# Infini-attention with a gated mix: when the next segment's x is asked for, and a new table by slot

## The chip, the cores and the metric

The kernel runs on one core of one Trainium2 chip. The metric is the time of one execution on the device in microseconds (us), as the median of several runs; the kernel before has 1017.42 us (three runs, 1017.11 to 1020.25).

## The reference

Two branches A and B with weights of their own read the same x (2048 tokens, 640 wide, 32 heads of 20) and are mixed by a gate for each token. Each branch is attention over four segments of 512 tokens, with a memory that is carried from segment to segment:

```python
phi = lambda t: jnp.where(t > 0, t + 1.0, jnp.exp(t))
for s in range(N):                      # N = 4 segments
    qs, ks, vs = q[:, :, s], k[:, :, s], v[:, :, s]
    logits = jnp.einsum("bhqd,bhkd->bhqk", qs, ks) * scale + mask
    a_dot = jnp.einsum("bhqk,bhkd->bhqd", _softmax(logits, axis=-1), vs)
    pq = phi(qs)
    a_mem = einsum(pq, M) / (einsum(pq, z)[..., None] + 1e-6)
    outs.append(g * a_mem + (1.0 - g) * a_dot)
    M = M + jnp.einsum("bhld,bhle->bhde", phi(ks), vs)
    z = z + phi(ks).sum over l
...
g = _sigmoid((x * gate_w).sum(-1, keepdims=True))
return g * a + (1 - g) * b              # a, b: the branches' outs @ wo
```

The causal mask adds -1e9 above the diagonal. q, k and v are x times 640 x 640 weights.

## The kernel before

**Stages.** A stage t = 0 to 7 is one branch of one segment: segment t // 2, branch A for even t and B for odd t. In each stage the products q, k (five blocks of 128 output columns each, m = 0 to 4), v (two halves of 320 columns, called m = 0 and m = 4) and o (five blocks) are to be computed, in three parts each (high by high, low by high, high by low), all at line 769. x and every weight are therefore split into a high and a low part: ACT copies the high part (x at L582, weights at L537, v's weights at L511), and POOL, or VectorE at the start, subtracts for the low one (L586, L539, L514). v's weights come in three pieces through the three tiles `wst`.

**Attention units.** Each stage has eight units of four heads, 64 in all (i). For a unit, q and k rows are loaded into one of four pairs of tiles (`qst`, `kst`, L1163). L1205 are the scores whose row maxima VectorE takes (L1192); VectorE writes the maxima as two parts (`mt`, L1218 and L1219), TensorE transposes them (L1232), ACT copies them (`mr`, L1249), and a DMA puts them below q (L1244). L1297 are the transposed scores with the maxima subtracted, ACT takes Exp (L1289), POOL clears what the mask hides (L1290), and L1317 multiplies by v. L879 reads the memory and L961 updates it; L921 are transposes.

**How TensorE is shared.** A matmul over 64 rows takes one half of the array, and two of them, one on each half, run beside each other. L1317 takes the whole array, with four products beside each other in column groups.

**What sets the order.** Nothing is decided on the chip. A planner in Python keeps a clock with a length for every operation, a queue for each engine (A is ACT, D is VectorE, G is POOL, S is SyncE, which issues all DMAs) and pools of tiles (34 `row` tiles, eight `bank` tiles in PSUM, three `wst` tiles), and writes each engine's instructions down in the order in which they come out; an engine then runs them in that order, and waits where one isn't ready. The attention units come slot by slot: a slot i issues five T steps of unit i (`t_unit`, L1297) and five S steps of unit i + 2 (`s_unit`, L1205). Between them the product jobs fill TensorE, in the order of a list `jobs`. For stages after the first, a window's jobs are k2, v0, q3, k3, q4, k4, v4, and then the next stage's q0, k0, q1, k1, the o products of the stage before, and the next stage's q2.

**The table.** `RULES` has an entry for some slots; a slot without one goes on with the last. An entry holds the order of S and T steps, and seven numbers: `span` (the share of the slot's time in which its steps are laid), `calm` (how much work VectorE may have waiting for lesser units to start), `lag` (how long the second half of a unit waits for its first), `room` (row tiles that must be free for Exp's outputs), `hold`, `wait` and `wait2` (how long other units wait).

**The requests.** `begin` is called as a job starts. It asks for weights four jobs ahead, and at one place for the next segment's x (`want_x`, five transfers from `in_xT`, L592; each needs three free row tiles and leaves two spare). `fill_gen` asks at another place for x by token (`token_gate`, four transfers from `in_x` into `wst` tiles, L635), of which VectorE makes the gates of the segment (L625).

Of the kernel before, what the change touches and what calls it, by code (L numbers as in the profile page):

```python
# [42 lines left out]
def tile_gated_mix_infini_attn(  # L43
# [44 lines left out]


    RULES = {  # L90
# [56 lines left out]
    }  # L147
    rule = {}
    DONE = {"A": 0.27, "D": 0.26, "G": 0.22, "S": 0.0}
# [428 lines left out]
    def want_x(s, k):  # L578

        def got(hi, lo, st):  # L580
            def landed():
                put("A", 0.515, lambda: nc.scalar.copy(hi, r32(st)), low, prio=6)  # L582

            def low():
                e, eng, cost = ("D", nc.vector, 0.66) if s == 0 else ("G", nc.gpsimd, 1.25)
                put(e, cost, lambda: eng.tensor_tensor(out=lo, in0=r32(st), in1=r32(hi), op=ALU.subtract), end, prio=3)  # L586

            def end():
                big.give(st)
                xs[s, k] = (hi, lo)  # L590

            dma(0.87, lambda: nc.sync.dma_start(  # L592
                out=r32(st), in_=xT[P * k:P * (k + 1), L * s:L * (s + 1)]), landed, prio=need[job_index[2 * s, "q", 0]] - 4 * (s > 0), lat=1.2 if s else 1.1)

        big.want((F32R, F32R, F32), got, prio=4, spare=SPARE if s else 0)
# [75 lines left out]
    def ask_gates(*ts):  # L671
        gates_asked.extend(ts)
        for t in list(gates_asked):
            if t // 2 in gates_ready:
                gates_asked.remove(t)
                gq_store.want(1, lambda q, t=t: put("G", 1.3 if t == 7 else 0.7, lambda: gates(t, q), prio=2), prio=t)
# [843 lines left out]
    def begin(i):  # L1520
        t, kind, m = jobs[i]
        for j in range(i, i + AHEAD + 1):
            stage(j)
        if kind == "q" and m == 2 and t > 1:
            ask_gates(t)
        if kind == "v" and m == 4 and t % 2 and t < 7:
            for k in range(KT):
                want_x(t // 2 + 1, k)

    def fill_gen():  # L1530
        for i, (t, kind, m) in enumerate(jobs):
            begin(i)
            if i == 4:
                for n in range(NB):
                    token_gate(n)
            if kind == "v" and m == 0 and t % 2 and t < 7:
                for n in range(NB * (t // 2 + 1), NB * (t // 2 + 2)):
                    token_gate(n)
            if i < len(HEAD0):
                yield from job_head() if i == 0 else ()  # L1540
                continue
            yield from {"q": lambda: job_qk(t, kind, m), "k": lambda: job_qk(t, kind, m),
                        "v": lambda: job_v(t, m // 4), "o": lambda: job_o(t, m),
                        "early": lambda: job_early(t, m), "last": lambda: job_last(t)}[kind]()

    fill = fill_gen()
    filled = [0.0]
    over = [False]
# [241 lines left out]
```

## Time and profile before

| | us |
|---|---|
| median of the runs | 1017.42 |
| the profiled execution's own time | 1018.35 |
| its span in the trace | 1016.6 |
| TensorE busy with matmuls | 1002.2 (99%) |
| TensorE loading weights (beside them) | 855.9 (84%) |
| VectorE busy | 814.0 (80%) |
| ACT busy | 654.1 (64%) |
| POOL busy | 596.3 (59%) |
| bytes moved | 241.99 MB, 238 GB/s in the mean |

"Busy" is the time in which at least one instruction of the engine was under way, so TensorE is also busy where one half of the array idles. The chain of waits goes back from the last instruction to whatever released each one; shares of it say which work set the end. In lists of waits the three numbers are the sum in us, how often, and the longest. In groups of instructions they are the busy time in us and the mean in ns, then the idle time before them.

### The profile page before, as it was taken

What the parts mean: (1) busy time and instruction counts of PE and PEld (TensorE: products, weight loads), DVE (VectorE), ACT (ScalarE), POOL (GpSimd) and SP (SyncE); (2) the same over time, 40 slices, a digit from 0 to 9 for tenths busy, and PEclk for the clock granted to TensorE, in tenths of its full rate; (3) what the DMA queues carried; (4) which work ended last, traced back from release to release, by engine and by line L of the source; (5) the groups of instructions that cost most, each with busy time, mean ns of one, the idle gap of its engine ahead of it and who ended that gap; (6) DMA issues with size and microseconds to landing.
All of it is one profiled execution on the core that took longest, in us unless ns stands there. A gap on an engine that the chain in (4) does not pass through costs nothing.

```text
span 1016.6 us, 30789 instructions
## 1 busy us (share of the span) xinstructions
PE 1002.2 (99%) x11260; PEld 855.9 (84%) x11260; DVE 814.0 (80%) x2732; ACT 654.1 (64%) x1281; POOL 596.3 (59%) x972
## 2 busy tenths in 40 slices
PE   9999999999999999999999999999999999999998
PEld 7988888878898887998889987788887877888875
DVE  5698889887698769886779888689668898779864
ACT  5376676677657567666766566666666556676572
POOL 4455547765466656757555565656664556656471
PEclk9999999999999999999999999999999999999999
DMA  7998989898797788966787588797667978767431
GB/s 255 307 313 261 290 251 317 253 299 258 243 295 230 238 251 257 296 185 198 217 260 241 181 262 245 219 321 252 176 200 205 288 206 264 238 199 246 139 113 53
DMA packets 148887, 241.99 MB, mean 238 GB/s; under 512 B 13216, under 2 KB 46144, under 8 KB 148416
## 3 DMA queue, kind: packets, MB, share of 16 engines
q1 hardware_dynamic: 148736, 240.03, 77.0%
q8 instruction: 89, 1.46, 0.6%
q14 instruction: 62, 0.51, 0.2%
HBM read 150.83 MB, written 94.65 MB: 241 GB/s over the span
## 4 chain that ended last, share of the span: by engine, by line
PE 86%; DVE 7%; DMA 3%; ACT 1%; issue 1%; SPq 0%; POOL 0%; DVEq 0%; ACTq 0%
PE bank L769 51%; PE bank L1317 12%; PE bank L1297 7%; PE bank L1205 7%; PE bank L961 3%; PE bank L879 3%; PE bank L921 2%; DVE bank L1192 2%; DMA row<-rowg 1%; PE bank L1232 1%; DVE mt L1218 1%; DVE mt L1219 1%; DVE row L735 1%; DVE row L1494 1%; ACT p L1289 1%
## 5 line engine op out<-in xcount | busy, mean ns | idle before, releaser
L1192 DVE CUSTOM_DVE_ANT_0 bank<-bank,tri 128x384 f32<-128x384 f32 (+3 forms) x1024 | 474.5, 519 | 125.3 <-PE bank L1205 99.4
L769 PE MATMUL bank<-row,wh 64*128 64x512 f32 x2308 | 517.6, 404 | 1.1 <-DMA qst<-qd 0.8
L1289 ACT ACTIVATE p<-bank 128x512 f32<-128x512 f32 x566 | 311.1, 600 | 127.2 <-PE bank L1297 95.5
L1290 POOL TENSOR_SCALAR_AFFINE_SELECT p<-p 128x128 f32<-128x128 f32 (+1 forms) x566 | 214.0, 386 | 237.7 <-ACT p L1289 225.4
L769 PEld LDWEIGHTS bank<-row,wh 64*128 64x128 f32 x2308 | 324.8, 185 | 12.3 <-DVE mx L1192 1.2
L769 PE MATMUL bank<-row,wl 64*128 64x512 f32 x1154 | 296.7, 399 | 0.0
L539 POOL TENSOR_TENSOR wl<-wst,wh 128x640 fp32r<-128x640 f32 x115 | 179.4, 1565 | 52.7 <-ACT wh L537 51.9
L1297 PE MATMUL bank<-qst,kst 62*128 62x128 f32 (+3 forms) x1024 | 179.7, 318 | 2.7 <-DVE row L1494 0.7
L1205 PE MATMUL bank<-kst,qst 60*128 60x128 f32 (+3 forms) x1024 | 179.0, 317 | 1.7 <-DVE row L719 0.7
L769 PEld LDWEIGHTS bank<-row,wl 64*128 64x128 f32 x1154 | 174.1, 186 | 5.0
L769 PE MATMUL bank<-wvh,row 64*128 64x320 f32 x1280 | 175.4, 312 | 0.0
L769 PEld LDWEIGHTS bank<-wvh,row 64*128 64x128 f32 x1280 | 148.1, 185 | 1.7 <-ACT p L1289 0.3
L1317 PE MATMUL bank<-p,vst 128*32 128x512 f32 (+3 forms) x1888 | 144.7, 424 | 0.0
L1192 DVE DVE_READ_ACCUMULATOR2_ANT mx<- 128x1 f32 x1024 | 144.6, 141 | 0.0
L1297 PEld LDWEIGHTS bank<-qst,kst 62*128 62x128 f32 x1024 | 132.1, 186 | 11.8 <-DVE mx L1192 1.8
L1205 PEld LDWEIGHTS bank<-kst,qst 60*128 60x128 f32 x1024 | 131.2, 186 | 8.2 <-DVE mx L1192 1.8
L1317 PEld LDWEIGHTS bank<-p,vst 128*32 128x32 f32 x1888 | 58.5, 110 | 83.0 <-issue 59.5
L769 PE MATMUL bank<-wvl,row 64*128 64x320 f32 x640 | 103.4, 311 | 0.0
L537 ACT CAST wh<-wst 128x640 fp32r<-128x640 f32 x119 | 86.3, 740 | 23.5 <-PE bank L769 13.1
L1347 ACT COPY row<-bank 128x512 f32<-128x512 f32 x61 | 35.9, 589 | 95.6 <-PE bank L1317 84.5
L769 PEld LDWEIGHTS bank<-wvl,row 64*128 64x128 f32 x640 | 82.9, 185 | 0.1
L514 POOL TENSOR_TENSOR wvl<-wst,wvh 128x640 fp32r<-128x640 f32 (+1 forms) x48 | 64.0, 1337 | 22.6 <-ACT wvh L511 22.5
(117 smaller groups left out, 1255.2 us busy)
## 6 DMA issues: line engine op xcount, KB each, us to landing
qst<-qd SPq DMA_DIRECT2D x128, 240.0 KB
kst<-kd SPq DMA_DIRECT2D x128, 240.0 KB
qd<-row SPq DMA_DIRECT2D x40, 512.0 KB
kd<-row SPq DMA_DIRECT2D x40, 512.0 KB
dots<-row SPq DMA_DIRECT2D x56, 256.0 KB
wst<-wmix SPq DMA_DIRECT2D x35, 320.0 KB
row<-dots SPq DMA_DIRECT2D x42, 256.0 KB
qd<-row SPq DMA_DIRECT2D x40, 256.0 KB
```

Source lines behind the costliest of these rows:

```text
L514: put("G", 0.77 * n, lambda: nc.gpsimd.tensor_tensor(out=wl[:, a:b, :], in0=w3, in1=r32(wh[:, a:b, :]), op=ALU.subtract), end, prio=4)
L537: put("A", 0.625, lambda: nc.scalar.copy(wh, w3), lambda: put(lo_eng, lo_cost, lambda: lo.tensor_tensor(out=wl, in0=w3, in1=r32(wh), op=AL ...
L539: lambda: lo.tensor_tensor(out=wl, in0=w3, in1=r32(wh), op=ALU.subtract), end, prio=3), prio=6)
L769: return nc.tensor.matmul(bank_of, lhsT=w[ROWS[half]], rhs=x_[ROWS[half]], start=start, stop=stop)
L879: return nc.tensor.matmul(pm[:, a - h0:c - h0, :].rearrange("p h e -> p (h e)"), lhsT=r32(pqTs[t, m][ROWS[half], P * n:P * (n + 1)]), rhs= ...
L1192: put("D", w / 960.0 + 0.105, lambda: nc.vector.tensor_tensor_reduce(out=sc[:, off:off + w], in0=sc[:, off:off + w], in1=tri[:, L - w:], s ...
L1205: lane_ops[half].append((mm(w), lambda pair=pair, qb=qb, off=off, w=w, r=r, sc=sc: nc.tensor.matmul(sc[:, off:off + w], lhsT=q[r, pair, P ...
L1289: put("A", 0.483, lambda: nc.scalar.activation(pt, sc, AF.Exp, scale=SCALE), lambda: (bank.give(sc), put("G", 0.15 + 0.105 * len(todo), la ...
L1290: "G", 0.15 + 0.105 * len(todo), lambda: nc.gpsimd.affine_select(out=blocks, in_=blocks, pattern=[[0, len(todo)], [1, P]], base=0, channel ...
L1297: lane_ops[half].append((mm(w), lambda pair=pair, kb=kb, off=off, w=w, r=r, sc=sc: nc.tensor.matmul(sc[:, off:off + w], lhsT=k[r, pair, P ...
L1317: nc.tensor.matmul(po[32 * j:32 * j + 32, P * kb:], lhsT=vst[t % 2][:, kb, h * E1:h * E1 + 32], rhs=pts[i, n, f][0][:, off:off + w], start ...
L1347: either(0.483, lambda: nc.scalar.copy(r32(oT), po), 0.605, lambda: nc.vector.tensor_copy(r32(oT), po), end, 2)
```

## The change

Two conditions and the whole table:

```diff
     RULES = {
-        0: "TSTSTSTSTS 1.033 2.38 0.30 8 0.0 1.6 1.41",
-        1: "TSTSTSTSTS 0.953 3.71 0.30 8 0.0 2.99 0.36",
-        2: "TTSTSTSTSS 1.010 3.52 0.30 4 0.0 2.63 0.25",
...
+        0: "TTSTSTSTSS 1.010 2.38 0.30 8 0.0 1.6 0.71",
+        1: "TSTTSSTSTS 1.010 2.38 0.30 8 0.0 1.6 0.38",
+        3: "TTSTSTSTSS 0.936 2.38 0.30 8 0.0 1.6 1.55",
...
     }
...
-        if kind == "v" and m == 4 and t % 2 and t < 7:
+        if kind == "q" and m == 4 and t % 2 and t < 7:
             for k in range(KT):
                 want_x(t // 2 + 1, k)
...
-            if kind == "v" and m == 0 and t % 2 and t < 7:
+            if kind == "v" and m == 4 and t % 2 == 0 and t < 6:
                 for n in range(NB * (t // 2 + 1), NB * (t // 2 + 2)):
                     token_gate(n)
```

x of the next segment is asked for two jobs earlier (q4 instead of v4 of branch B's stage), and x by token at the second half of v in branch A's stage instead of the first half of v in branch B's. Lines behind the table stand three further down (L592 becomes L595). The number of instructions of each kind is the same on TensorE and SyncE; on the others a few evacuations change their engine. Three places show how the order moves; names carry the number of the tile.

The first is SyncE's queue in stage 5, where x of segment 3 is asked for. Before:

```order
L521 DMA wst0_142<-in_b_wv_dram 128x640
L521 DMA wst2_144<-in_b_wv_dram 128x640
L748 DMA kd5_110<-row25_12547_10686 128x2x512
L748 DMA kd5_110<-row20_12548_10687 128x512
L521 DMA wst0_142<-in_b_wv_dram 128x320
L592 DMA row30_12683_10795<-in_xT_dram 128x512
L592 DMA row31_12689_10799<-in_xT_dram 128x512
L592 DMA row10_12694_10802<-in_xT_dram 128x512
L592 DMA row5_12699_10805<-in_xT_dram 128x512
L1163 DMA qst3_83<-qd5_102 60x2x512 x2
```

After the change:

```order
L524 DMA wst1_143<-in_b_wv_dram 128x640
L524 DMA wst2_144<-in_b_wv_dram 128x640
L595 DMA row27_12554_10711<-in_xT_dram 128x512
L1247 DMA qst0_80<-mr1_162 2x8x128 x2
L595 DMA row5_12560_10715<-in_xT_dram 128x512
L595 DMA row16_12565_10718<-in_xT_dram 128x512
L595 DMA row8_12570_10721<-in_xT_dram 128x512
L1166 DMA qst3_83<-qd5_102 60x2x512 x2
L1166 DMA kst3_87<-kd5_110 60x2x512 x2
L524 DMA wst1_143<-in_b_wv_dram 128x320
```

The third piece of v's weights (128x320) stood ahead of four x transfers; now it stands behind them and behind four loads of q and k rows.

The second is SyncE's queue where x by token for segment 3 is fetched: before, in stage 5, places 497 to 506 of the queue.

```order
L635 DMA wst1_143<-in_x_dram 128x640
L748 DMA qd5_102<-row29_12109_10288 128x2x512
L748 DMA qd5_102<-row5_12110_10289 128x512
L1362 DMA dots4_121<-row19_12189_10350 128x512
L635 DMA wst0_142<-in_x_dram 128x640
L1244 DMA qst3_83<-mr0_161 2x8x128 x2
L635 DMA wst1_143<-in_x_dram 128x640
L635 DMA wst0_142<-in_x_dram 128x640
L1163 DMA qst2_82<-qd5_102 60x2x512 x2
L1163 DMA kst2_86<-kd5_110 60x2x512 x2
```

After the change, in stage 4, places 450 to 458; the fourth of these transfers stands at place 466.

```order
L638 DMA wst0_142<-in_x_dram 128x640
L638 DMA wst2_144<-in_x_dram 128x640
L1166 DMA qst1_81<-qd4_101 60x2x512 x2
L1166 DMA kst1_85<-kd4_109 60x2x512 x2
L638 DMA wst1_143<-in_x_dram 128x640
L551 DMA wst0_142<-wmix1_131 128x5x128
L1247 DMA qst3_83<-mr0_161 2x8x128 x2
L1365 DMA dots4_121<-row11_10929_9279 128x512
L551 DMA wst2_144<-wmix1_131 128x5x128
```

They now take the `wst` tiles ahead of the o products' weights, and not ahead of a q and k load that waits behind them.

The third is ACT's queue at the cast of v's third piece in stage 5. Before:

```order
L511 CAST wvh_153<-wst2_144 128x640
L511 CAST wvh_153<-wst0_142 128x320
L1347 COPY row20_12752_10849<-bank5_139 128x512
L1249 CAST mr1_162<-bank1_135 32x128
L582 CAST row26_12681_10793<-row30_12683_10795 128x512
```

After:

```order
L585 CAST row28_12558_10713<-row5_12560_10715 128x512
L585 CAST row15_12563_10716<-row16_12565_10718 128x512
L585 CAST row12_12568_10719<-row8_12570_10721 128x512
L756 CAST row31_12795_10879<-bank0_134 128x512
L726 ACTIVATE row20_12797_10881<-bank0_134 128x512
L1292 ACTIVATE p4_12817_10894<-bank5_139 128x512
L1292 ACTIVATE p5_12818_10895<-bank3_137 128x512
L514 CAST wvh_153<-wst1_143 128x320
L1252 CAST mr0_161<-bank7_141 32x128
```

The third piece's cast stood ahead of x's casts and now stands behind four of them (the first is five places further up); the copy of the next maxima (`mr`) stands behind it in both.

103 rows, old and new, of the table RULES are left out of this document.

## The prediction

> **What bounds the kernel now.** I read the page first: the engines' busy shares, the rows of slices, and the chain that ended last.
>
> ```profile
> span 1016.6 us, 30789 instructions
> PE 1002.2 (99%) x11260; PEld 855.9 (84%) x11260; DVE 814.0 (80%) x2732; ACT 654.1 (64%) x1281; POOL 596.3 (59%) x972
> PE   9999999999999999999999999999999999999998
> PEclk9999999999999999999999999999999999999999
> DMA packets 148887, 241.99 MB, mean 238 GB/s; under 512 B 13216, under 2 KB 46144, under 8 KB 148416
> PE 86%; DVE 7%; DMA 3%; ACT 1%; issue 1%; SPq 0%; POOL 0%; DVEq 0%; ACTq 0%
> PE bank L769 51%; PE bank L1317 12%; PE bank L1297 7%; PE bank L1205 7%; PE bank L961 3%; PE bank L879 3%; PE bank L921 2%; DVE bank L1192 2%; DMA row<-rowg 1%; PE bank L1232 1%; DVE mt L1218 1%; DVE mt L1219 1%; DVE row L735 1%; DVE row L1494 1%; ACT p L1289 1%
> ```
>
> TensorE works in every slice at the full granted clock, and 86% of the chain is its own work. The change alters no product, so that work stays; only what stands between the products can move. How much is that? The windows at both ends, and TensorE's waits:
>
> ```profile
> 0.00:25.00 25.00, 22.73 (x139) 18.25 (x141) 12.32 (x25) 14.36 (x28) 10.65 (x25) 1.00 0.76 255
> 1000.00:1017.00 17.00, 12.22 (x86) 9.15 (x78) 7.96 (x14) 1.76 (x3) 0.00 (x0) 0.98 0.22 78
> PE bank L1232 <- DVE mt L1219: 1.6, 4, 0.5
> PE bank L769 <- DMA qst<-qd: 0.8, 1, 0.8
> PE bank L1205 <- DVE row L719: 0.7, 1, 0.7
> PE bank L1297 <- DVE row L1494: 0.7, 2, 0.4
> PE bank L1297 <- ACT mr L1249: 0.5, 1, 0.5
> ```
>
> The second number of a window is PE's busy time. Of 1016.6 - 1002.2 = 14.4 us without a product, 25.00 - 22.73 = 2.3 lie before 25 us and 16.6 - 12.22 = 4.4 behind 1000 us, which leaves 7.7 us in the stream, in pieces of at most 0.8 us, mostly behind VectorE. No row names x or its split as what a product waited for. So the asked-for x is no bottleneck that the change could remove; what it can do is to deal the stream's 7.7 us, and the idle halves of the array, anew.
>
> **The change, part by part.** Nothing is added or removed on TensorE, SyncE or the DMA queues: 9732 matmuls and 940 transfers stand in both programs. Three things move.
>
> *1. x of the next segment.* It is asked for at q's fifth product of an odd t instead of at v's second half. The order shows what that makes of SyncE's queue at segments 2 and 3: the x transfers followed all three pieces of v's weights, and now three or four of them stand ahead of the third piece. Was x late before?
>
> ```profile
> L586 POOL TENSOR_TENSOR row<-row,row x5: 1268/1297/1759, 165.5 to 176.3; 128x512 fp32r<-128x512 f32 x5
> L769 PE MATMUL bank<-wvh,row x80: 301/306/412, 159.7 to 176.4; 64*128 64x320 f32 x80
> ```
>
> These are the tile views of the first such place (150 to 185 us; "first and last start"). The last split of x starts at 176.3 and takes 1.3 us, so x is whole at 177.6; the last v product with wvh starts at 176.4, and products with wvl follow it, of which half as many are in the program. So x was just in time even here, and TensorE has attention units to run meanwhile. The earlier ask is worth 0. If that cover were gone, it would be worth 1.2 us (177.6 - 176.4) at each of three segments, 3.6 us; I keep that as the end for a gain.
>
> *2. x by token for the gates.* Three of the four transfers for segments 2 and 3 are issued some 40 issues earlier, and spread over more of the queue.
>
> ```profile
> L625 DVE CUSTOM_DVE_ANT_0 wst<-wst,gw 128x640 f32<-128x640 f32 x16 | 13.8, 866 | 2.5 <-DMA wst<-in_x_dram 2.5
> ```
>
> Each costs VectorE 0.87 us whenever it comes, so the work is unchanged, and its waits (2.5 us) lie beside TensorE's products. Cost 0; if the 0.8 us that TensorE waited for a q load (above) came of the crowded queue, it would be -0.8.
>
> *3. The table.* It moves nearly every instruction. I price three effects.
>
> First, the engines' loads. The planner chooses the engine of some evacuations by load: eight q or k pieces change from Exp on ACT with two VectorE passes (L718, L719) to Relu and Exp on ACT with one (L725), seven copies of L937 and L1347 move from ACT to VectorE, and one weighing (L1427) to POOL.
>
> ```profile
> L718 DVE TENSOR_SCALAR bank<-bank 128x512 f32<-128x512 f32 x35 | 24.8, 710 | 0.0
> L719 DVE TENSOR_TENSOR row<-bank,row 128x512 f32<-128x512 f32 x35 | 23.8, 683 | 0.2
> L725 DVE SCALAR_TENSOR_TENSOR row<-bank,row 128x512 f32<-128x512 f32 x25 | 16.9, 677 | 0.4 <-POOL p L1290 0.4
> L1347 DVE COPY row<-bank 128x512 f32<-128x512 f32 x3 | 2.1, 692 | 0.4 <-PE bank L1317 0.4
> L1427 DVE TENSOR_TENSOR row<-row,row 128x512 f32<-128x512 f32 x17 | 20.9, 1257 | 0.0
> ```
>
> VectorE: -8 x (0.710 + 0.683 - 0.677) + 7 x 0.692 - 1.257 = -2.1 us of 814. That is 0.3% of an engine that is 80% busy: 0 for the time.
>
> Second, the packing. Row-half matmuls of the two halves run beside each other, and each L1317 unit needs the whole array, so both halves must have ended. A half that carries less between two such units idles. The chain of waits gives the price: eight half matmuls of 512 columns, four on each half, in 0.93 us, so 0.23 us on one's own half, and in proportion for narrower ones (twice that for L879 and L961, which run in two passes).
>
> ```profile
> 990.06 0.93 PE bank L769 x8
> 991.00 2.29 PE bank L1317 x32
> ```
>
> Which half a matmul uses is in its operands, in the program and not in a row. Summed over the 64 stretches, half the difference of the two halves is 9.9 us before and 8.7 now: **-1.2 us**. Bounds: nothing, if the lighter half's idle time was waiting for data anyway, and the whole 9.9 - 8.7.
>
> Third, the waits, which mostly come out of one mechanism. VectorE turns the row maxima into two parts (L1218, L1219) for TensorE's transposes (L1232), and these tiny operations are sometimes held:
>
> ```profile
> L1218 DVE CAST mt<-mx x64: 161/175/1465, 40.7 to 983.3; 128x16 fp32r<-128x16 f32 x64
> L1219 DVE TENSOR_TENSOR mt<-mx,mt x64: 174/176/1525, 41.0 to 983.5; 128x16 fp32r<-128x16 f32 x64
> L1219 DVE TENSOR_TENSOR mt<-mx,mt 128x16 fp32r<-128x16 f32 x64 | 26.4, 413 | 2.2
> L1218 DVE CAST mt<-mx 128x16 fp32r<-128x16 f32 x64 | 23.2, 362 | 0.8
> 783.72 1.55 POOL L539 TENSOR_TENSOR wl<-wst,wh 128x640 fp32r<-128x640 f32 x1 [0.33 <-ACT wh L537]
> 785.23 0.88 POOL L514 TENSOR_TENSOR wvl<-wst,wvh 128x320 fp32r<-128x320 f32 x1
> 784.16 1.14 DVE L1218 CAST mt<-mx 128x16 fp32r<-128x16 f32 x1
> 785.33 0.80 DVE L1219 TENSOR_TENSOR mt<-mx,mt 128x16 fp32r<-128x16 f32 x1
> 786.79 0.44 PE L1205 MATMUL bank<-kst,qst 60*128 60x384 f32 x1 [0.70 <-DVE row L719]
> ```
>
> Minimum, median and maximum stand first. The median is 0.175 us and the maximum 1.5; in the timeline both end with the POOL subtraction that was running (785.27 and 786.11), the L719 behind them is late, and TensorE waits 0.70 us. In sum VectorE is held (26.4 + 23.2) - 128 x 0.175 = 27 us, and the chain carries these two lines with 1% each, some 20 us. A new order deals these meetings anew: the same 128 operations against the same POOL work, so the same number is the likeliest. I change one thing: stretches where less than 3.5 us of products stand between a unit's last L1205 and its L1232 fall from 7 to 1, and four such transposes waited 1.6 us, 0.4 each; I take one wait off, **-0.4 us** (bounds 0 and -1.6).
>
> The sum is -1.6 us against the profiled execution, 1018.35 us with its span of 1016.6. That execution lies 0.93 us above the median 1017.42 of the runs, so the forecast is 1017.42 - 1.6 = **1015.8 us**.
>
> **The rivals.** *A better deal.* Fewer of the small operations meet POOL's long ones. A third fewer takes a third of the chain's 20 us, 6.6, unless something else is late next; half of that, 3.3, gives 1012.5, and the whole 1015.8 - 6.6 = 1009.2. For it: 20 us are there to be had. Against it: nothing in the change looks at POOL, and as many may be added. [...]
>
> *Slower: v's third piece comes late.* With x ahead of it in SyncE's queue, that piece lands later, and TensorE stands at v's second half.
>
> ```profile
> 650.08 0.33 SPq L521 DMA_DIRECT2D wst<-in_b_wv_dram  x1
> 654.97 0.46 ACT L511 CAST wvh<-wst 128x320 fp32r<-128x320 f32 x1 [2.37 <-DMA wst<-in_b_wv_dram]
> L514 POOL TENSOR_TENSOR wvl<-wst,wvh x1: 862/862/862, 655.5 to 655.5; 128x320 fp32r<-128x320 f32 x1
> L769 PE MATMUL bank<-wvh,row x16: 299/306/365, 660.4 to 663.4; 64*128 64x320 f32 x16
> ACT wvh L511 <- DMA wst<-in_b_wv_dram: 5.3, 4, 2.4
> row<-in_xT_dram SPq DMA_DIRECT2D x20, 256.0 KB
> qst<-qd SPq DMA_DIRECT2D x128, 240.0 KB
> ```
>
> Even before, ACT waited 2.37 us for it, with the copy for the next row of maxima (L1249) behind. The split ended at 656.4 and v's first product came at 660.4: 4.0 us of cover. Now four x transfers and four q and k loads stand between (1.98 MB as the rows count, 2.03 million bytes), 8.5 us at 238 GB/s. If all of it counts, TensorE loses 8.5 - 4.0 = 4.5 us there; with segment 2, where three x transfers stand ahead, taken alike, 9.0 us, so up to 1024.8; half of it gives 1020.3. It decides from 4.0 us of added delay on. Against it: the order also puts the cast later and other ACT work ahead of it, and units lie between. [...]
>
> *The change doesn't do what it says.* x waits for three free rows wherever it is asked for; in segment 3 its first issue stands at place 516 before and 517 now. Then the table alone acts: the forecast's time.
>
> **How the numbers follow.** Forecast (1013 to 1018.5, with the last rival) 0.47, the better deal 0.31, v's piece late 0.22. The range takes in 1009.2 below and reaches to 1023 above, short of the full price of 1024.8, which needs both places to lose all cover: 1009 to 1023. A measurement of this kernel can tell about 0.3% (3.05 us) from no change, so the bounds are 1014.4 and 1020.5. Faster: 0.31 and 0.08 of the forecast's, 0.39. Slower: most of v's rival, 0.21. The same: 0.40.
>
> **What would show it.** Right: PE busy stays at 1002 within 2 us, the long tail of L1218 and L1219 (maximum 1.5 us, means 362 and 413 ns) is about as heavy, the waits on L1219 are three or fewer, and TensorE waits for neither wvh, wvl nor x. The better deal: both means under 330 ns. The slower rival: ACT's wait for v's pieces well above 5.3 us, with L769 waiting for wvh or wvl. Wrong altogether: a wait of some us at one place, or another granted clock.

## The result and the profile after

The changed kernel takes **1029.14 us** (median of four runs, 1027.58 to 1035.83) against 1017.29 us of the kernel before on the same chip: slower by 1.2%, ratio 1.0122 [1.0074, 1.017]. The prediction said 1015.8 us and 1009 to 1023; the time lies 6 us above the range. Of all runs below, one (the longest of after_split, 1040.73 us) was in a slower state and is left out of its median and ratio. The profiled execution took 1029.75 us, its span is 1028.0 us, 11.4 us more than before.

The page of the changed kernel, first its busy times, then the row of the granted clock:

```profile
PE 1004.5 (98%) x11260; PEld 857.0 (83%) x11260; DVE 822.0 (80%) x2730; ACT 654.9 (64%) x1282; POOL 595.7 (58%) x973
...
PEclk9999999999999999999999999999999999999999
```

TensorE's instructions are the same in number, VectorE is busy 8.0 us longer although it has two instructions fewer. The rows to set beside those of before are the list of TensorE's waits, and VectorE's two operations on `mt` (lines stand three further down: L1221 and L1222 are L1218 and L1219 of before), first with minimum, median and maximum, then as groups:

```profile
PE bank L1235 <- DVE mt L1222: 8.9, 8, 2.1
PE bank L1300 <- DVE mx L1195: 2.4, 2, 2.2
PE bank L924 <- DVE row L722: 1.6, 2, 1.1
```
```profile
L1221 DVE CAST mt<-mx x64: 159/254/3331, 41.6 to 993.1; 128x16 fp32r<-128x16 f32 x64
L1222 DVE TENSOR_TENSOR mt<-mx,mt x64: 174/176/1568, 41.8 to 994.6; 128x16 fp32r<-128x16 f32 x64
```
```profile
L1221 DVE CAST mt<-mx 128x16 fp32r<-128x16 f32 x64 | 30.4, 475 | 1.0
L1222 DVE TENSOR_TENSOR mt<-mx,mt 128x16 fp32r<-128x16 f32 x64 | 26.5, 413 | 2.2
```

"Held" is the time beyond the 0.175 us of an undisturbed one. The 128 operations are held for (30.4 + 26.5) - 128 x 0.175 = 34.5 us, 27 before, and the longest takes 3.3 us, 1.5 before. TensorE's waits on `mt` grew from four with 1.6 us to eight with 8.9 us. All rows of that list sum to 9.4 us before and 18.5 us after. One place in the timeline of all engines shows how such a wait comes about (start, duration, engine, line):

```profile
444.57 3.10 POOL L542 TENSOR_TENSOR wl<-wst,wh 128x640 fp32r<-128x640 f32 x2
444.60 1.55 DVE L1221 CAST mt<-mx 128x16 fp32r<-128x16 f32 x1
...
446.18 1.52 DVE L1222 TENSOR_TENSOR mt<-mx,mt 128x16 fp32r<-128x16 f32 x1
447.62 0.68 DVE L738 TENSOR_TENSOR row<-bank,row 128x512 fp32r<-128x512 f32 x1
...
447.75 0.23 PE L1235 MATMUL bank<-ident,mt 64*32 64x64 f32 x1 [2.11 <-DVE mt L1222]
```

The cast (1.55 us) ends with GpSimd's first subtraction, the subtraction on VectorE (1.52 us) with the second, and TensorE stands for 2.11 us. And then the clock. The row above shows only nines, since a slice is 25.7 us long, but the mean granted clock of the run is 0.994. Here are windows of the changed kernel, 3.41 us each, with the busy time (and count) of PE, PEld, DVE, ACT and POOL, then the granted clock, the DMA share and GB/s:

```profile
186.22:189.63 3.41, 1.32 (x15) 1.23 (x16) 3.41 (x17) 1.63 (x4) 1.64 (x2) 1.00 0.42 156
189.63:193.04 3.41, 3.41 (x25) 3.41 (x22) 2.92 (x11) 3.41 (x8) 2.25 (x3) 0.50 0.98 271
421.75:425.16 3.41, 1.65 (x37) 1.29 (x30) 3.38 (x5) 0.00 (x0) 2.02 (x2) 1.00 0.99 258
425.16:428.57 3.41, 3.41 (x51) 3.41 (x49) 3.38 (x4) 2.01 (x5) 0.59 (x2) 1.00 0.65 208
445.64:449.05 3.41, 1.30 (x18) 1.19 (x20) 3.38 (x5) 0.91 (x2) 2.01 (x2) 1.00 0.96 353
449.05:452.46 3.41, 3.41 (x25) 3.07 (x24) 2.82 (x5) 1.83 (x4) 1.03 (x3) 0.50 0.83 277
705.05:708.46 3.41, 1.81 (x31) 0.94 (x25) 3.08 (x4) 0.59 (x1) 1.78 (x2) 1.00 1.08 329
708.46:711.87 3.41, 3.41 (x32) 3.41 (x32) 2.58 (x4) 1.49 (x4) 1.33 (x2) 0.50 0.58 222
```

Three times (189.6, 449.0, 708.5) a window with stalls is followed by one at half clock, called a dip below; the trace of before has none, its clock is 1.00 up to 1016.2 us, just ahead of the end. From the granted clock, a dip is estimated to cost at most 3.41 x 0.5 = 1.7 us, the three 5.1 us. The span's 11.4 us are 9.1 us more without a product and 2.3 us more of busy time, the dips among it: so either a dip costs less than 1.7 us, or busy time was gained elsewhere. This one trace can't tell which; the runs of five_held below speak for the first. Nobody waited for v's weights or x on TensorE, and ACT's waits for v's pieces fell, against 5.3 and 2.4 before:

```profile
ACT wvh L514 <- DMA wst<-in_b_wv_dram: 4.3, 6, 0.9
```

### The profile page after: what moved, and what is told of

The parts are those of the page before. It is cut to its first block, busy times and chain, and to the rows that moved or that the text cites. A ratio compares the mean times of both kernels' runs of the same rounds, so it can differ in the third digit from the quotient of the medians.

```text
span 1028.0 us, 30780 instructions
## 1 busy us (share of the span) xinstructions
PE 1004.5 (98%) x11260; PEld 857.0 (83%) x11260; DVE 822.0 (80%) x2730; ACT 654.9 (64%) x1282; POOL 595.7 (58%) x973
## 5 line engine op out<-in xcount | busy, mean ns | idle before, releaser
L1195 DVE CUSTOM_DVE_ANT_0 bank<-bank,tri 128x256 f32<-128x256 f32 (+3 forms) x1024 | 474.7, 518 | 137.6 <-PE bank L1208 110.2
L772 PE MATMUL bank<-row,wh 64*128 64x512 f32 x2308 | 512.0, 405 | 0.0
L1292 ACT ACTIVATE p<-bank 128x512 f32<-128x512 f32 x576 | 317.4, 600 | 147.1 <-PE bank L1300 116.6
L1293 POOL TENSOR_SCALAR_AFFINE_SELECT p<-p 128x256 f32<-128x256 f32 (+1 forms) x576 | 217.5, 387 | 261.0 <-ACT p L1292 250.1
L772 PE MATMUL bank<-row,wl 64*128 64x512 f32 x1154 | 300.5, 401 | 0.0
L1208 PE MATMUL bank<-kst,qst 60*128 60x384 f32 (+3 forms) x1024 | 180.6, 317 | 1.9 <-DVE O L899 0.6
L772 PE MATMUL bank<-wvh,row 64*128 64x320 f32 x1280 | 180.0, 314 | 0.7 <-DVE mx L1195 0.7
L1300 PE MATMUL bank<-qst,kst 62*128 62x512 f32 (+3 forms) x1024 | 175.7, 318 | 3.4 <-DVE mx L1195 2.4
L1208 PEld LDWEIGHTS bank<-kst,qst 60*128 60x128 f32 x1024 | 135.2, 186 | 7.2 <-DVE mx L1195 1.3
L1300 PEld LDWEIGHTS bank<-qst,kst 62*128 62x128 f32 x1024 | 131.2, 186 | 11.7 <-DVE mx L1195 4.8
L540 ACT CAST wh<-wst 128x640 fp32r<-128x640 f32 x119 | 86.4, 743 | 31.0 <-PE bank L772 18.9
L1350 ACT COPY row<-bank 128x512 f32<-128x512 f32 x55 | 32.4, 589 | 83.8 <-PE bank L1320 74.7
```

Of the source, the lines that this page charges most:

```text
L540: put("A", 0.625, lambda: nc.scalar.copy(wh, w3), lambda: put(lo_eng, lo_cost, lambda: lo.tensor_tensor(out=wl, in0=w3, in1=r32(wh), op=AL ...
L772: return nc.tensor.matmul(bank_of, lhsT=w[ROWS[half]], rhs=x_[ROWS[half]], start=start, stop=stop)
L1195: put("D", w / 960.0 + 0.105, lambda: nc.vector.tensor_tensor_reduce(out=sc[:, off:off + w], in0=sc[:, off:off + w], in1=tri[:, L - w:], s ...
L1208: lane_ops[half].append((mm(w), lambda pair=pair, qb=qb, off=off, w=w, r=r, sc=sc: nc.tensor.matmul(sc[:, off:off + w], lhsT=q[r, pair, P ...
L1292: put("A", 0.483, lambda: nc.scalar.activation(pt, sc, AF.Exp, scale=SCALE), lambda: (bank.give(sc), put("G", 0.15 + 0.105 * len(todo), la ...
L1293: "G", 0.15 + 0.105 * len(todo), lambda: nc.gpsimd.affine_select(out=blocks, in_=blocks, pattern=[[0, len(todo)], [1, P]], base=0, channel ...
```

## The experiments

Medians in us; the ratio is to the kernel before in the same comparison.

| kernel | median | ratio, 95% |
|---|---|---|
| requests_only | 1068.88 | 1.0523 [1.0477, 1.0568] |
| table_only | 1088.49 | 1.0705 [1.0686, 1.0724] |
| before_mx | 1009.74 | 0.9938 [0.992, 0.9956] |
| after_mx | 1010.05 | 0.9939 [0.9924, 0.9954] |
| before_plain | 1071.97 | 1.0541 [1.0503, 1.0579] |
| after_plain | 1077.32 | 1.0587 [1.0563, 1.0611] |
| before_split | 1015.40 | 0.9982 [0.9972, 0.9992] |
| after_split | 1028.61 | 1.0095 [1.0056, 1.0134] |
| before_nudge | 1059.87 | 1.0425 [1.0395, 1.0455] |
| before_ghost | 1016.26 | 0.9983 [0.9971, 0.9996] |
| after_ghost | 1030.14 | 1.0122 [1.0098, 1.0146] |
| before_stall | 1034.76 | 1.017 [1.015, 1.0191] |
| after_fill | 1011.40 | 0.9931 [0.9917, 0.9945] |
| before_fill | 1008.26 | 0.9913 [0.99, 0.9927] |
| five_free | 1017.89 | 0.9996 [0.9975, 1.0017] |
| five_held | 1020.96 | 1.0032 [1.0016, 1.0048] |

### One half of the change alone

requests_only has the two conditions with the old table, table_only the new table with the old conditions.

> The kernel before with both new conditions (x at the fifth product of q, x by token at the second half of v) and the old table. Theory H (holds): the change costs time because its order brings VectorE's small mt operations, which were held 27 us before and 34.5 us after, behind GpSimd's long subtractions at places where TensorE waits for them (the waits on mt grew from 2.1 + 0 to 8.9 + 2.4 us), and because three stalls of over 2.2 us are each followed by half clock for 3.41 us. By H the requests by themselves cost nothing; but they too deal the order anew, so the time goes with the held time on mt: about 1017 plus 0.9 us for each us by which the held time exceeds 27, that is 1012 to 1024, and without a dip of the clock not over 1020. Theory R (requests): the transfers asked for earlier stand in the way of others; by R this kernel has nearly the whole loss, 1026 to 1030, and TensorE waits for wvh, wvl, a row of x or VectorE waits for x by token.

> The changed kernel's table with the old two conditions. Theory H: again another order, its time goes with its held time on mt and with its dips of the clock: 1012 to 1030, and the relation of requests_only (0.9 us for each us held over 27, plus 1.7 us for each dip) gives it within 3 us. Theory R: the table costs nothing, so 1014 to 1018.5, whatever is held. A third, T (the table itself is slow, by which half of the array or which engine gets the work): 1026 to 1030 although held time and dips are as before.

Both are far slower than the whole change, so the parts do not add: +52 and +72 us against +11.9 together. The relation with the held time failed outright: `mt` was held for 27.5 and 31.0 us. R failed too, since TensorE waits for no transfer of weights or x. The page of requests_only and the first rows of TensorE's waits in it:

```profile
PE 1037.8 (98%) x11260; PEld 880.3 (83%) x11260; DVE 814.2 (77%) x2730; ACT 652.6 (61%) x1283; POOL 592.5 (56%) x972
```
```profile
PE bank L1232 <- DVE mt L1219: 12.0, 10, 3.4
PE bank L1317 <- DVE mx L1192: 2.2, 1, 2.2
PE bank L340 <- DVE qst L344: 1.5, 1, 1.5
```

TensorE is *busy* 35.6 us longer with the same 11260 instructions, while all its listed waits sum to 20.5 us. Busy counts when either half of the array works, and one half often goes on alone: with the half of each matmul taken from the program, the traces have one half alone at work for 78.0 us in requests_only and 87.0 in table_only, against 28.2 before and 28.9 in the changed kernel. Half of the 49.8 us more, 24.9, is most of the 35.6; four windows at half clock add up to 6.8. The packing as the prediction counted it is only a part of this: by the program, the halves between two L1317 units are out of balance by 18.9 and 21.6 us (9.9 before, 8.7 in the changed kernel), 9.0 and 11.7 more than before; for what the halves wait otherwise was not traced.

### What a table is worth without the requests that it was made for

A neutral table of one row, with the old and the new conditions (`before_plain`, `after_plain`), and then one row's order changed in the kernel before:

```diff
     RULES = {
+        0: "TSTSTSTSTS 1.010 2.38 0.30 8 0.0 1.6 1",
-...
```
```diff
-        5: "TSTSTSTSTS 1.010 3.77 0.30 8 0.0 2.17 0.73",
+        5: "TTSTSTSTSS 1.010 3.77 0.30 8 0.0 2.17 0.73",
```

> The kernel before with a table of one row, the neutral one (TSTSTSTSTS 1.010 2.38 0.30 8 0.0 1.6 1), for all slots: an order that the table was fitted to no requests. The runs with half of the change were 52 and 71 us slower though neither TensorE's waits for transfers nor the held time on mt (24.5 and 28 us) had grown by that; in their place half matmuls stood idle beside the other half's work (packing by the program 18.9 and 21.6 us against 9.9 and 8.7). Theory F (fit): a table is worth its gain only with the requests that it was made for, and either half of the change makes an order for which its rows are any rows. By F the neutral table is as slow as they: 1060 to 1095. Rival: the mixtures were slow for a reason of their own (the old rows with the new requests delay one transfer), and the neutral table gives 1020 to 1045.

> The two new conditions with the neutral one-row table. Theory F with the prediction's step that the requests are worth nothing by themselves: the same as the kernel before with the neutral table within 10 us (two orders drawn from one planner). Theory R (the requests themselves cost): slower than it by 20 us or more, with TensorE or VectorE waiting for x, wvh or wvl.

> The kernel before with one letter order changed in one row of its table (slot 5: TTSTSTSTSS for TSTSTSTSTS); requests as before. Neither half of the change is in it. Theory F (a table fits one order only): from slot 5 on the later rows meet another state, so the loss is of the size of the two mixtures and of the neutral tables, 1045 to 1095, by half matmuls that stand beside nothing. Rival (the mixtures lost through the requests): one row's order is worth a few us, 1012 to 1027.

1071.97, 1077.32 and 1059.87 us: theory F holds. A table is a list of answers to one course of the planner; what changed that course early turned its other rows into any rows, and in these five kernels 42 to 72 us were lost, whether it was one row's order or a request. So a part of this change can't be priced by undoing it: 5.3 us between the two neutral tables is little beside what one row's order moves, and is no price of the requests.

### VectorE's two operations on mt taken out

```diff
...
-        def parts():
-            nc.vector.tensor_copy(mt[:, :, 0, :], m)
-            nc.vector.tensor_tensor(out=mt[:, :, 1, :], in0=m, in1=r32(mt[:, :, 0, :]), op=ALU.subtract)
-
-        put("D", 0.22, parts, lambda: m_ready(i), prio=0)
+        mts[i] = mx[i]
+        put("D", 0.22, lambda: None, lambda: m_ready(i), prio=0)
...
```

With them goes the low part of the maxima: the transposes (L1232), ScalarE's copy and the transfer below q carry 16 rows in place of 32.

> The kernel before with VectorE's two operations on mt (L1218, L1219) taken out: TensorE transposes the maxima themselves (16 columns in place of 32), ScalarE's copy rounds them, and one row in place of two stands below q. It leaves out the low part of the row maximum, which the quotient does not see. The order of all other instructions is that of the kernel before. Theory H: the 27 us of holds and 22.4 us of the operations' own time leave VectorE (814 to about 764 us busy) and TensorE's waits on mt (2.1 us) and a part of those behind VectorE go: 1009 to 1016, with no row of TensorE waiting for mx over 3 us. Theory R says nothing of it: 1015 to 1017.5, since 2.1 us of waits are all that can go.

> The changed kernel with the same two operations taken out, and all else in the changed kernel's order. Theory H: the stalls at 185.7 stay in part (there two lines of the weighing and GpSimd's parts of it also stand), those at 294.8, 422.1, 445.4, 617.3 and 706 go, and with them at least two of the three dips of the clock: within 3 us of before_mx, 1011 to 1019. Theory R or T: the loss of 11.9 us stays for the most part, 1024 to 1029, since only what stands on mt (11.3 us of waits at most) could go and something else is late next.

1009.74 and 1010.05 us: 11.9 us of difference shrink to 0.3, with every other instruction in its old order. **The loss stands on these 128 operations and what hangs on them**, and both kernels gain by their removal, so before_mx and after_mx beat the kernel before and the changed one. One dip, at 188.6 us, is left in after_mx, as expected: there VectorE's weighing (L1430 in the changed kernel, L1423 here; 1.8 us for one against 0.7 at its shortest) meets GpSimd's.

### Waiting for mt, late VectorE, or only more to do?

The ghosts put the two operations back, read by nobody. The fills put two reductions of the same maxima in their places:

```diff
-            nc.vector.tensor_copy(mt[:, :, 0, :], m)
-            nc.vector.tensor_tensor(out=mt[:, :, 1, :], in0=m, in1=r32(mt[:, :, 0, :]), op=ALU.subtract)
+            nc.vector.tensor_reduce(out=mt[:, :, 0, 0:1], in_=m, axis=mybir.AxisListType.X, op=ALU.max)
+            nc.vector.tensor_reduce(out=mt[:, :, 1, 0:1], in_=m, axis=mybir.AxisListType.X, op=ALU.max)
```

> The kernel before_mx with the two operations on mt put back on VectorE, in the places of the kernel before, but read by nobody: TensorE transposes the maxima themselves as in before_mx. VectorE so has its 22 us and its holds again. If the holds cost time because TensorE waits for mt: 1009 to 1012, as before_mx. If they cost it because VectorE's later work comes late: 1015 to 1018, as the kernel before.

> The same for the changed kernel: after_mx with L1221 and L1222 put back, read by nobody. If TensorE's waits for mt (11.3 us in the profile) are the loss: 1010 to 1014. If VectorE's backlog behind a held operation is it: 1024 to 1030 with the same dips of the clock. From the stalls at 445 and 706 us, where the products behind the transposes wait too for VectorE's next operation, I expect between the two, 1014 to 1022, nearer to the first.

> after_ghost with its two unread operations exchanged for two unread reductions of the same 128x16 maxima, in the same places of the same order: VectorE is given about the same own time (22 us in 128 operations), but in a form that may not meet GpSimd (one input, no cast, no second input). If the holds behind GpSimd make the loss (theory H as left by the ghosts): the reductions have no long tail (maximum under 0.4 us), and the time is 1009 to 1014, as after_mx. If the operations' own time on VectorE makes it: 1026 to 1032, as after_ghost.

> The same for before_ghost. Holds: 1008 to 1012.5, as before_mx; own time: 1014 to 1018, as before_ghost.

after_ghost has the whole loss again (1030.14), which rules out the expectation's "nearer to the first", and before_ghost nearly the whole time of the kernel before (1016.26). So the smaller transposes, copies and transfers, which the ghosts share with the mx kernels, are not what was gained there, and TensorE's wait for `mt` was only the name under which the loss showed: in after_ghost TensorE's waits sum to 18.8 us, 18.5 in the changed kernel, and none is on `mt`. The timeline of after_ghost, at the place of the third dip:

```profile
703.26 3.06 POOL L542 TENSOR_TENSOR wl<-wst,wh 128x640 fp32r<-128x640 f32 x2 [0.51 <-DMA qst<-qd]
...
703.62 1.23 DVE L1221 CAST mt<-mx 128x16 fp32r<-128x16 f32 x1
704.88 1.47 DVE L1222 TENSOR_TENSOR mt<-mx,mt 128x16 fp32r<-128x16 f32 x1
...
706.27 0.69 DVE L721 TENSOR_SCALAR bank<-bank 128x512 f32<-128x512 f32 x1
707.05 0.69 DVE L722 TENSOR_TENSOR row<-bank,row 128x512 f32<-128x512 f32 x1
...
707.80 0.47 PE L924 MATMUL bank<-ident,O 64*128 64x64 f32 x8 [1.82 <-DVE row L722]
```

The transposes no longer wait, and TensorE stands all the same: for L722, which VectorE reaches late. Whether the operations' own length or the holds do this, the fills answer (minimum, median and maximum, after_ghost first, then after_fill):

```profile
L1221 DVE CAST mt<-mx x64: 161/207/3784, 41.4 to 993.9; 128x16 fp32r<-128x16 f32 x64
```
```profile
L1221 DVE TENSOR_REDUCE mt<-mx x64: 156/168/173, 41.2 to 975.6; 128x2 f32<-128x16 f32 x64
L1222 DVE TENSOR_REDUCE mt<-mx x64: 152/160/164, 41.3 to 975.7; 128x2 f32<-128x16 f32 x64
```

The reductions are as long as an undisturbed cast, and none is held (173 ns at most, against 3784 for the cast); after_fill takes 1011.40 us, before_fill 1008.26. With the holds gone the two orders lie 3.1 us apart in place of 11.9: **the loss is held time, all but 3.1 us** (after_fill still has the dip near 188 us, before_fill has none).

The holds of the order before cost 1016.26 - 1008.26 = 8.0 us for 26.6 us held in before_ghost, 0.30 each. Those of the changed order cost 1030.14 - 1011.40 = 18.7 us for 37.9 us held, 0.49 each; two dips more than in after_fill are in that price.

### Five units

Why is a held microsecond dearer in the changed order? The reductions stand in units 18, 25, 26, 27 and 43 alone (five_free, the diff to after_ghost), or with `not in` everywhere else (five_held):

```diff
+            if i in (18, 25, 26, 27, 43):
+                for c in range(2):
+                    nc.vector.tensor_reduce(out=mt[:, :, c, 0:1].bitcast(F32), in_=m, axis=mybir.AxisListType.X, op=ALU.max)
+                return
```

> after_ghost with the unread operations exchanged for the reductions in five units alone (18, 25, 26, 27 and 43, held for 2.4, 2.0, 3.6, 2.8 and 2.4 us there, 13.1 of 37.9 us; 2.4, 2.0, 3.2, 2.7 and 2.4 us in the changed kernel). If the loss goes with the amount of held time (18.7 us between after_ghost and after_fill for 37.9 us held, 0.49 us for each): 1030.1 - 6.4 = 1022 to 1026. If it goes with the place (VectorE's slack takes up a hold of up to some 1.5 us, and two of the three dips of the clock follow these units): 1012 to 1018.

> The complement: the unread cast and subtraction in these five units alone, reductions in the other 59. Amount: 1011.4 + 6.4 = 1016 to 1020. Place: 1023 to 1028, with two dips of the clock at some 450 and 708 us.

five_free gets 12.2 of the 18.7 us back, as "place" had it; five_held pays 1020.96 - 1011.40 = 9.6 us, between what the two theories gave. Its ten operations, and two windows behind unit 18:

```profile
L1225 DVE CAST mt<-mx x5: 826/1295/2252, 292.2 to 699.0; 128x16 fp32r<-128x16 f32 x5
L1226 DVE TENSOR_TENSOR mt<-mx,mt x5: 175/1473/1540, 293.5 to 700.2; 128x16 fp32r<-128x16 f32 x5
```
```profile
293.74:297.15 3.41, 1.46 (x19) 1.12 (x17) 3.41 (x5) 0.87 (x2) 1.53 (x2) 1.00 0.70 263
297.15:300.56 3.41, 3.41 (x33) 3.41 (x32) 3.02 (x5) 0.74 (x2) 1.98 (x6) 0.50 0.10 38
```

They are held for 10.3 us: 0.93 us for each, dips included (this profile has windows at half clock behind three of the units, at 297, 447 and 703 us). In five_free the others are held for 26.3 us and cost 1017.89 - 1011.40 = 6.5 us: 0.25 each, about the price of the order before (0.30), and rough, since its runs spread from 1012.04 to 1021.85 us. So five units of 64 cost nearly all of their held time, and the rest in the mean a quarter. The kind of hold does not tell the two apart: in the five both operations meet GpSimd's subtractions one behind the other, or the cast meets several, but units 6 and 10 of five_free are held in the same way for 2.4 and 2.1 us. In after_ghost TensorE stood for 1.6 and 1.9 us behind units 6 and 19, which are not among the five.

The runs of five_held also show what a dip is worth. The three with the highest mean clock (0.998) take 1019.3 us in the mean, the three with the lowest (0.991 to 0.992) 1022.7 us: 3.4 us for some 6.8 us of clock time that was not granted. By this estimate a dip costs about half of its 1.7 us.

In the order before, three units were held for over 2 us (the longest 2.4), and no dip followed; in the changed kernel five, up to 3.2.

### Shorter GpSimd instructions

Each subtraction of a weight in five pieces, and in the same way v's pieces in blocks of 160 columns:

```diff
...
-                    lambda: lo.tensor_tensor(out=wl, in0=w3, in1=r32(wh), op=ALU.subtract), end, prio=3), prio=6)
+                    lambda: [lo.tensor_tensor(out=wl[:, k, :], in0=w3[:, k, :], in1=r32(wh[:, k, :]), op=ALU.subtract)
+                             for k in range(KT)][0], end, prio=3), prio=6)
```

> The kernel before with GpSimd's subtractions for the weights (L539, L514: 1.57 and up to 1.55 us) cut into five, and two or four, pieces each, in the same place of the same order. If VectorE's tiny mt operation gets in when the running GpSimd instruction ends, the longest hold falls from 1.5 to about 0.4 us, the held time from 27 to under 12 us, and the time to 1009 to 1015, at the price of GpSimd's fixed time for 163 x 3 or 4 more instructions. [...]

> The same cut of L542 and L517 in the changed kernel. [...]

If GpSimd goes on from piece to piece, 1015 to 1020 us were expected of before_split and 1025 to 1033 of after_split; if VectorE gets in between, 1012 to 1020 of after_split. before_split takes 1015.40 us and after_split 1028.61 (1022.25 to 1030.05), not clearly less than the changed kernel with 1029.14. GpSimd is busy for 674.8 us in before_split, 596.3 before. The timeline of after_split, GpSimd and then VectorE (its lines stand two further down):

```profile
418.50 6.32 POOL L543 TENSOR_TENSOR wl<-wst,wh 128x128 fp32r<-128x128 f32 x15
```
```profile
418.42 6.43 DVE L1223 CAST mt<-mx 128x16 fp32r<-128x16 f32 x1
424.88 0.17 DVE L1224 TENSOR_TENSOR mt<-mx,mt 128x16 fp32r<-128x16 f32 x1
```

A cast of sixteen columns stood for 6.43 us through fifteen pieces (6.32 us): here GpSimd went on from piece to piece. In before_split few were held (three units over 1 us, 13 in the kernel before), but those for up to 3.5 us, 22.4 us in all.

### The clock

before_stall is before_mx with seven growing heaps of fills on VectorE ahead of a unit's transposes:

```diff
+        late = {6: 8, 14: 12, 22: 16, 30: 20, 38: 24, 46: 28, 54: 32}.get(i, 0)
...
+            for _ in range(late):
+                nc.vector.memset(scr, 0.0)
+            if late:
+                nc.vector.tensor_copy(m, mx[i])
```

> The kernel before_mx with VectorE kept busy ahead of the transposes of seven units (8, 12, 16, 20, 24, 28 and 32 fills of a 128x128 scratch tile, and a copy of the maxima that TensorE then transposes): TensorE stalls of growing length, far from one another, in an order that has otherwise no dip of the clock. If a window of 3.41 us in which TensorE works less than some 0.4 of the time is followed by one at half clock, the short stalls leave no dip and the long ones (from 2.2 us on) one or two each, each dip some 1.7 us on top of the stall. Rival: the dips of the changed kernel were of another cause (their places lie 259.4 us apart), then the long stalls here leave no dip, or one at another place.

TensorE's waits in it, and windows around the second long stall:

```profile
PE bank L1236 <- DVE mlate L1223: 13.8, 4, 5.3
PE bank L1205 <- DVE mx L1192: 5.9, 2, 5.3
```
```profile
614.52:617.93 3.41, 1.83 (x32) 0.71 (x24) 2.19 (x15) 0.58 (x1) 1.00 (x2) 1.00 1.01 293
617.93:621.35 3.42, 0.51 (x3) 0.22 (x3) 2.46 (x14) 0.00 (x0) 0.00 (x0) 1.00 0.80 306
621.35:624.76 3.41, 3.39 (x20) 3.33 (x22) 1.64 (x8) 1.58 (x4) 0.59 (x2) 0.50 0.01 2
```

In TensorE's records there are four stalls of over 3 us (3.1, 4.5, 5.4 and 5.3); each is followed by half clock, the first two for one window and the others for two. The shorter ones (0.8 to 1.4 us) are followed by none. So here stalls of 3.1 us and more made such dips by themselves, in an order that has none of its own. Where they begin is not settled: windows with 1.30 and 1.32 us of work led to a dip, one with 1.65 and one with 1.83 did not, and the changed kernel's at 705 us, with 1.81, did. Part of the answer is that PE's busy time counts either half of the array. With the time in which one half works alone counted as half, the window at 705 us has 1.69 us of work; in eleven traces of these runs with dips each of the 24 windows at full clock with at most 1.6 us was then followed by half clock, and the least that was not had 1.65. Above that some were, so this is no threshold.

## Why the prediction was wrong, point by point

**The products** were right in their number, 11260 matmuls. TensorE is 1004.5 us busy, 0.5 us outside the "within 2 us of 1002"; the 2.3 us more lie within what the dips can cost (up to 5.1 us).

**The requests at nothing**: no row of the changed kernel speaks against it; TensorE waits for no wvh, wvl or x, and ACT waits less for v's pieces. The slower rival (v's third piece late) did not come. Shown directly it is not: any request moved alone re-deals the order, which costs 42 us and more.

**The table's engine loads** came as counted, but VectorE's busy time rose by 8.0 us where -2.1 stood: +7.2 us by the holds on `mt` (27.2 to 34.4) and 1.2 us each at L1377 and L625, which only took longer. With the operations on `mt` gone, before_mx and after_mx have 770.9 and 770.2 us. **The packing** of -1.2 us can't be seen: one half alone works for 28.9 us, 28.2 before, and with the holds gone the two orders differ by +0.3 us (mx) and +3.1 us (fill, with one dip). Its price of L879 and L961, twice the proportion, was too low: the trace before has 528 and 480 records for 264 and 240 matmuls of the program, two for each, and on one half a record follows the one before by 0.11 us for 84 columns (701 us) and 0.125 us for 147 (151 us), where 0.23 us for 512 gives 0.04 and 0.07.

**The waits** are the step that failed: "the same 128 operations against the same POOL work, so the same number is the likeliest", with one wait less. The mechanism was the one that the prediction named, and its number of meetings did not stay: 34.5 us for 27, eight waits on `mt` with 8.9 us for four with 1.6. Three mistakes lie in that step. It gave a better deal 0.31 and a worse one nothing, though it says itself that "as many may be added". It priced the holds by the chain's share, "some 20 us" of 27, when before_ghost and before_fill show 8.0, so the mean price was over twice too high. Those 20 us came of shares rounded to 1%: the chain has L1218 with 0.8% and L1219 with no more, 16 us at most, and the operations' own time is in them. The dear holds are few; whether VectorE's slack in a place decides that is likely, but not shown. And it had no term for the clock, up to 5.1 us, which windows with stalls of up to 2.2 us set off and which the profile before couldn't show, as it has none; the last line's "another granted clock" did name it.

**"The table alone acts"**, the rival that the change does little, would have meant the same time for table_only as for both: it is 59 us slower.

**What stays open**: which row of the table or which request put GpSimd's subtractions beside these five units can't be told by undoing one of them. And what let the order before take holds of 2.1 to 2.4 us without a long stall was not tested unit by unit.

## What to carry to other kernels

A hand-fitted table of scheduling numbers belongs to one course of the scheduler: judge a change in such a kernel as a whole new draw, and give a worse deal a chance of its own: here all six orders other than the one before were slower. A tiny instruction on an engine that has little slack is best given a form that the runs show not to be held, as the reductions here (173 ns at most), or left out: 128 operations of 0.175 us cost 8 to 19 us by their holds, and before_mx, without them and without the low part of the maxima, beats both kernels with 1009.74 us. When an operation is held, look for who comes late behind it, not only for who waits for its result.

## What the runs showed of the hardware

A held VectorE instruction did not always get in when GpSimd's running instruction ended: a cast stood 3.33 us through three subtractions of 1.5 us (the changed kernel at 420 us), and 6.43 us through fifteen short ones (after_split at 418 us). Counted over the operations on `mt` that took more than 0.23 us, in the kernel before, the changed one and the two with the split subtractions: at each of the 72 ends of a GpSimd instruction behind which GpSimd paused, VectorE got in. Where GpSimd's next instruction followed at once, VectorE came first at 45 of 53 ends in the first two, and at 89 of 190 in the two with the split subtractions.

TensorE's clock fell to half three times for 3.41 us in the changed kernel, after stalls that left TensorE 1.30 to 1.81 us of work in the 3.41 us ahead; it fell for 6.83 us in two places of before_stall and one of five_held.
